# Attention and two expert layers on one core: the ordering pass books "engine free" and "result visible" apart

## The chip, the cores and the metric

The kernel runs on one core of a Trainium2 chip. The metric is the device time of one execution in microseconds; of several runs the median is given. The engines are PE (matrix multiply, with its weight loads PEld), DVE (vector), ACT (scalar), POOL and SP (which issues all DMAs here).

## What is computed

```python
def reference(**kwargs):
    # attention: q, k, v of (4, 8, 576, 64), a memory M_prev (4, 8, 64, 64), z_prev, a gate beta per head
    scores = scale * q @ k^T;  scores = where(causal, -1e9, scores);  a = softmax(scores)
    local = a @ v
    q_p = phi(q)                       # phi(x) = where(x > 0, x, exp(x) - 1) + 1
    mem_out = (q_p @ M_prev) / (q_p . z_prev + 1e-6)
    attn = g * mem_out + (1 - g) * local          # g = sigmoid(beta)
    x = attn.transpose(0, 2, 1, 3).reshape(2304, 512)
    h = x @ moe_w_in;  x = (h * tanh(softplus(h))) @ moe_w_out        # 512 -> 2048 -> 512
    h = x @ moe2_w_in; return (h * cos(h)) @ moe2_w_out               # 512 -> 2048 -> 512
```

## The kernel before

Nothing in the kernel is issued in the order in which the text stands. Each piece of work is a task (`add`, line 163): the engine or engines that may run it, a cost in microseconds, a function that issues its instructions, the tasks it depends on, a rank, the buffers it takes and uses. `arrange` (line 176) then plays a clock forward over all tasks. Whenever an engine is free at the moment `now`, it gets the task of lowest rank that is ready by then; ACT is asked before DVE, so a task that may run on either ("act/dve", mostly copies out of PSUM) goes to whichever is free first in this plan. The list that comes out is issued task by task, and each engine runs its own instructions in exactly that order; semaphores make a task wait for what it needs. So the planner's costs never make an instruction faster; they decide order and engine.

In the plan before, a task that starts at `now` occupies its engine until `now + cost`, and whoever depends on it may start 0.1 us (`SEM`) later, whichever engine it ran on. Costs are written beside each task, as formulas in the number of columns n for copies: `c_act(n) = 0.19 + 0.00082 n` and `c_dve(n) = 0.11 + 0.00106 n`. Changing ACT's table costs `TABLE`, changing PE's kind of matmul costs `SWITCH`.

The work has these stages:

- Attention in 16 pairs of heads (`pair`, rank 100 m). For each pair PE transposes q and k through PSUM (L400, tiles ptq and ptk), ACT or DVE copies them (L315 for ACT; L317, L319 for DVE), PE makes scores (L491, L495), DVE takes row maxima (L520), ACT exponentials with their sums (L536), DVE sums and scales (L563, L564, L572), PE transposes the probabilities (L587, tile t), ACT or DVE copies them (tile PT), PE multiplies with v (L654), ACT or DVE copies the result (tile xs), and SP stores it.
- Each f32 weight is split into two parts in 64 decodes (`decode_w`, L125 to L142): four DVE instructions and one of ACT each.
- The first half of the first layer's hidden units runs in nine blocks of 256 tokens (`block0`, L759 and L802), which start as soon as their tokens' attention is stored. One PSUM tile (tag h) holds the hidden values.
- The second half of them, and then the second layer, run in blocks of 384 tokens (`late`, L887, L967, L969), six blocks each. They have three hidden PSUM tiles, and the second matmul of a unit is ranked two or five units behind the first (`LAG`).

Until the first block takes its hidden tile, the planner fills PE with dummy matmuls (L303) where PE would be idle and was idle too often in the time before. Every buffer class has a number of slots (`slots_of`); a task that takes a slot waits until the users of the slot's last holder have ended.

Of the kernel before, what the change touches and what calls it, by code (L numbers as in the profile page):

```python
# [29 lines left out]
def tile_kernel(ctx: ExitStack, tc: tile.TileContext, q, k, v, M_prev, z_prev, beta,  # L30
# [13 lines left out]
    LAG = (2, 5)  # L44
# [110 lines left out]
            made[cls] = self.n + 1  # L155

    class Task:
        __slots__ = ("eng", "cost", "fn", "deps", "rank", "takes", "func", "mode", "lag", "end", "n", "size", "on")

    tasks = []  # L160
    slots_of = {}

    def add(eng, cost, fn, deps=(), rank=0.0, takes=(), uses=(), func=None, mode=0, lag=0.0, size=0):
        t = Task()
        t.eng, t.cost, t.fn, t.rank, t.takes = eng.split("/"), cost, fn, rank, list(takes)
        t.func, t.mode, t.lag, t.end, t.on, t.size = func, mode, lag, None, None, size
        t.deps = [d for d in deps if d is not None]
        for b in (*takes, *uses):
            b.users.append(t)
        tasks.append(t)  # L170
        return t

    SEM, SWITCH, TABLE, WAIT = 0.1, 0.12, 1.3, 2.5
    RATE, LAND = 160.0, 2.0

    def arrange():
        outs = {}
        for t in tasks:
            t.n = len(t.deps)
            for d in t.deps:  # L180
                outs.setdefault(id(d), []).append(t)
        ready = {e: [] for e in ("pe", "act", "dve", "pool", "sp", "host")}
        seen = 0

        def put(t):
            nonlocal seen
            at = max((d.end + (d.lag if t.eng[0] != "host" else 0.0) + SEM for d in t.deps), default=0.0)
            for e in t.eng:
                ready[e].append((t.rank, seen, at, t))
            seen += 1  # L190

        for t in tasks:
            if not t.n:
                put(t)
        held = {c: [None] * n for c, n in slots_of.items()}
        turn = {c: 0 for c in slots_of}
        free = {e: 0.0 for e in ready}
        func, mode, moved = "exp", 0, 0.0
        done = deque()
        now, order, left = 0.0, [], len(tasks)  # L200


        def at_free(b):
            if b.cls != "misc" and b.n != turn[b.cls]:
                return None
            o = held[b.cls][turn[b.cls] % len(held[b.cls])]
            if o is None:
                return 0.0
            at = 0.0
            for u in o.users:  # L210
                if u.end is None:
                    return None
                at = max(at, u.end + SEM)
            return at

        while left:
            nxt = None

            def later(x):
                nonlocal nxt  # L220
                if nxt is None or x < nxt:
                    nxt = x

            for e in ready:
                if free[e] > now:
                    later(free[e])
                    continue
                best = None
                for r in ready[e]:
                    rank, k, at, t = r  # L230
                    if t.on is not None:
                        continue
                    for b in t.takes:
                        f = at_free(b)
                        if f is None:
                            at = None
                            break
                        at = max(at, f)
                    if at is None:
                        continue  # L240
                    if t.func and t.func != func:
                        at += WAIT if t.func == "mish" else 0.0
                    if at > now:
                        later(at)
                        continue
                    key = (t.func == "mish" != func, rank, k) if func != "mish" else (t.func != "mish", rank, k)
                    if best is None or key < best[0]:
                        best = (key, r)
                if best is None:
                    if e == "pe" and t_warm.on and not turn["h"]:  # L250
                        while done and done[0][1] < now - 3.4:
                            done.popleft()
                        if sum(y - max(x, now - 3.4) for x, y in done) < 0.75 * 3.4:
                            t = Task()
                            t.eng, t.cost, t.fn, t.on, t.end = ["pe"], 0.12, f_dummy, "pe", now + 0.12
                            free[e] = t.end
                            done.append((now, t.end))
                            order.append(t)
                            later(t.end)
                    continue  # L260
                r = best[1]
                t = r[3]
                cost = t.cost[t.eng.index(e)] if isinstance(t.cost, tuple) else t.cost
                if e == "act" and t.func and t.func != func:
                    cost, func = cost + TABLE, t.func
                if e == "pe":
                    cost, mode = cost + (SWITCH if t.mode != mode else 0.0), t.mode
                t.on, t.end = e, now + cost
                free[e] = t.end
                if e == "pe":  # L270
                    done.append((now, t.end))
                if t.size:
                    moved = max(moved, t.end) + t.size / RATE
                    t.lag = moved - t.end + LAND
                for b in t.takes:
                    held[b.cls][turn[b.cls] % len(held[b.cls])] = b
                    turn[b.cls] += 1
                for x in t.eng:
                    ready[x] = [q_ for q_ in ready[x] if q_[3] is not t]
                order.append(t)  # L280
                left -= 1
                for d in outs.get(id(t), ()):
                    d.n -= 1
                    if not d.n:
                        put(d)
                later(t.end)
                if e == "host":
                    later(now)
            if left:
                assert nxt is not None, [(e, r[0], r[3].fn.__name__, [(b.cls, b.n, turn[b.cls]) for b in r[3].takes]) for e in ready for r in ready[e]][:40]  # L290
                now = max(now, nxt)
        return order
# [53 lines left out]
    def pair(m):  # L346
# [4 lines left out]
        R = 100.0 * m  # L351
        B_ = {n: Buf(n) for n in ("q", "k", "v", "z", "mv", "mn", "ph", "qT", "kT", "kd", "PT", "xs")}
# [98 lines left out]
        RP = R + 12  # L451
# [2 lines left out]
        p2 = add("dve", 0.82, f_p2, [p1], RP, [B_["ph"]], [B_["mn"], B_["q"]])  # L454
        p3 = add("dve", 0.82, f_p3, [p2, dz], RP, [], [B_["mn"], B_["ph"], B_["z"]])
        bden = Buf("den")
        p4 = add("dve", 1.2, f_p4, [p3, t_ginv], RP, [bden], [B_["mn"]])

        def slot(x):
# [41 lines left out]
            for c, i in enumerate(SLOTS[x]):  # L503
# [35 lines left out]
                for part in range(2 if nk > 512 else 1):  # L539
                    for j in range(2):  # L540
                        w = (main, nk - main)[part]
                        takes = [] if fst or bx else [bp]
                        t_e = add("act", 0.48 + 0.00083 * w, lambda e, j=j, part=part, f=f_ex: f(e, j, part), [t_m, fst], S_ + 2,
                                  takes, [bn] + ([] if takes else [bp]) + [bs if part == 0 else bx], func="exp")
                        exps[i, j, part] = t_e
                        fst = fst or t_e

# [19 lines left out]
            for c, i in enumerate(SLOTS[x]):  # L567
                n_ = START[i] + ROWS[i]
                for j in range(2):
                    def f_sl(e, c=c, i=i, j=j):  # L570
                        p_ = d["p", i][:, j, D:]
                        nc.vector.tensor_scalar(out=p_, in0=p_, scalar1=s["sm"][:, c, j:j + 1], scalar2=None, op0=ALU.mult)  # L572

                    scaled[i, j] = add("dve", 0.1 + n_ / 1920, f_sl, [t_sm], S_ + 3, [], [bp])
                colsof[i] = cols[i]
                ptof[i] = bp

# [258 lines left out]
    def late(bi, s0):  # L836
        p, j = blocks[bi]
        m = p - 1
# [34 lines left out]
        for k_, f in enumerate(fs):  # L873
# [6 lines left out]
            for half in range(2):  # L880
                def f_1(e, half=half, f=f, q_=q_, s=s):
# [3 lines left out]
                    for c in (2 * half, 2 * half + 1):  # L885
                        for pi, (a, e_) in enumerate(PASSES):
                            nc.tensor.matmul(q_["h"], w[:, a, 0, c * P:(c + 1) * P], x[:, e_, c, :],  # L887
                                             start=c == 0 and pi == 0, stop=c == NKC - 1 and pi == 2)

                pe_.append(add("pe", 1.05, f_1, [sp[half], *w_ready[m, f, 0], t_host, *pe_[-1:]], R, [bh] if half == 0 else [],  # L890
                               [bx, bw] + ([bh] if half else [])))

            def Gt(q_=q_, s=s):
# [64 lines left out]
            for c in range(na):  # L958
                def f_2(e, c=c, k_=k_, f=f, q_=q_):
# [4 lines left out]
                    for pi, (a, e_) in enumerate(PASSES):  # L964
# [3 lines left out]
                        else:  # L968
                            nc.tensor.matmul(o, G[:, a, c * P:(c + 1) * P], w[:, e_, 1, :], start=st, stop=sp_)  # L969

                prev[c] = add("pe", 0.53 if m == 0 else 0.7, f_2, [t, prev[c], *w_ready[m, f, 1]], R + 10 * LAG[m] - 5,
                              [ba[c]] if k_ == 0 else [], [bG, bw] + ([ba[c]] if k_ else []))
        RF = R0 + 10.0 * len(fs) + 10 * LAG[m]
        outs = []
# [155 lines left out]
```

## Time and profile before

| | before |
|---|---|
| median of 3 runs | 1081.99 us (1081.27 to 1083.91) |
| span of the profiled execution | 1080.1 us |
| PE busy | 1053.2 us (98%) |
| PEld busy | 938.7 us (87%) |
| DVE busy | 761.6 us (71%) |
| ACT busy | 570.1 us (53%) |

The span runs from the first to the last instruction of the one profiled execution; the profile gives no other time for that execution. Busy shares are averages over stages with different limits, and matmuls are pipelined, with modelled ends, so a busy PE isn't at its peak.

### The profile page before, as it was taken

Reading aid. Unit: us, or ns where it says so; the run is one execution under the profiler, and the core shown is the slowest. Engines: PE = TensorE matmul, PEld = TensorE weight load, DVE = VectorE, ACT = ScalarE, POOL = GpSimd, SP = SyncE. Lnnn points to the kernel's source line nnn. Section 1 sums busy time; section 2 is a strip of 40 time slices with the busy share of each in tenths; the row PEclk is TensorE's granted clock in tenths of the full one; section 3 lists DMA queues with packets and bytes.
Section 4 is the critical chain, followed back from the end, with each engine's and each line's share of the span. In section 5 each row is a group of like instructions: output and inputs, shape, how many; then the busy total and the mean of one; then the engine's idle time right before and its main releaser. Section 6 shows DMA issues by size and latency. Waiting matters only on the chain.

```text
span 1080.1 us, 17930 instructions
## 1 busy us (share of the span) xinstructions
PE 1053.2 (98%) x6938; PEld 938.7 (87%) x6938; DVE 761.6 (71%) x1694; ACT 570.1 (53%) x1279; POOL 3.8 (0%) x19
## 2 busy tenths in 40 slices
PE   8898999999999999999999999999999999999998
PEld 5666778788877899989999999998999999999997
DVE  6999997886787568757552228887666676766664
ACT  4676675676676443433323234766555555555544
POOL 1000000000000000000000000000000000000000
PEclk9999999999999999999999999999999999999999
DMA  6455423222322165446352216211000010000000
GB/s 165 114 132 161 113 55 103 69 70 67 100 69 59 44 204 156 137 135 205 102 183 88 89 59 187 79 38 59 1 30 30 1 59 2 30 30 1 30 1 30
DMA packets 112853, 88.73 MB, mean 82 GB/s; under 512 B 65792, under 2 KB 103680, under 8 KB 112768
## 3 DMA queue, kind: packets, MB, share of 16 engines
q1 hardware_dynamic: 112768, 87.58, 27.1%
q8 instruction: 55, 0.90, 0.3%
q14 instruction: 30, 0.25, 0.1%
HBM read 68.69 MB, written 18.87 MB: 81 GB/s over the span
## 4 chain that ended last, share of the span: by engine, by line
PE 88%; DVE 7%; ACT 3%; issue 1%; POOL 0%; ACTq 0%; POOLq 0%; DVEq 0%
PE h L887 28%; PE acc L969 18%; PE acc L967 9%; PE h L759 9%; PE acc L802 9%; PE pv L654 5%; PE t L587 4%; PE s L491 3%; DVE nm L520 2%; DVE p L572 1%; PE warm L303 1%; ACT p L536 1%; PE ptq L400 1%; ACT PT L315 1%; PE ptk L400 1%
## 5 line engine op out<-in xcount | busy, mean ns | idle before, releaser
L887 PE MATMUL h<-x,w 128*128 128x384 f32 x1728 | 345.0, 337 | 1.6 <-ACT g L903 1.6
L887 PEld LDWEIGHTS h<-x,w 128*128 128x128 f32 x1728 | 307.4, 188 | 17.2 <-ACT g L903 1.8
L969 PE MATMUL acc<-w,G 128*128 128x512 f32 x864 | 228.4, 393 | 0.0
L969 PEld LDWEIGHTS acc<-w,G 128*128 128x128 f32 x864 | 160.0, 188 | 22.1
L954 DVE TENSOR_TENSOR G<-g,G 128x384 fp32r<-128x384 f32 x144 | 79.8, 555 | 100.2 <-ACT G L315 99.6
L759 PE MATMUL h<-x,w 128*128 128x256 f32 x864 | 127.7, 288 | 4.6 <-DVE g L317 4.2
L802 PE MATMUL acc<-G,w 128*128 128x256 f32 x864 | 129.7, 289 | 1.1 <-ACT o L315 0.7
L759 PEld LDWEIGHTS h<-x,w 128*128 128x128 f32 x864 | 111.4, 191 | 9.0 <-DVE g L317 5.2
L315 ACT ACTIVATE G<-g 128x384 fp32r<-128x384 f32 (+1 forms) x152 | 81.2, 535 | 66.6 <-DVE g L938 35.8
L802 PEld LDWEIGHTS acc<-G,w 128*128 128x128 f32 x864 | 111.9, 191 | 4.0 <-ACT o L315 1.4
L967 PE MATMUL acc<-G,w 128*128 128x384 f32 x576 | 112.6, 336 | 0.0
L536 ACT ACTIVATE p<-s,nm 128x64 f32<-128x64 f32 (+4 forms) x160 | 81.3, 515 | 40.0 <-DVE nm L520 26.2
L967 PEld LDWEIGHTS acc<-G,w 128*128 128x128 f32 x576 | 100.9, 188 | 0.0
L931 ACT ACTIVATE n<-n 128x384 f32<-128x384 f32 x96 | 49.9, 521 | 63.5 <-DVE n L927 63.5
L903 ACT ACTIVATE g<-h 128x384 f32<-128x384 f32 x48 | 23.4, 491 | 113.1 <-PE h L887 112.2
L587 PE MATMUL t<-ident,p 128*128 128x128 f32 (+1 forms) x480 | 73.7, 277 | 7.8 <-ACT PT L315 3.7
L520 DVE TENSOR_REDUCE nm<-s 128x2 f32<-128x1024 f32 (+4 forms) x80 | 62.2, 790 | 23.5 <-PE s L495 16.4
L915 DVE TENSOR_SCALAR u<-hs 128x384 f32<-128x384 f32 x96 | 34.5, 359 | 54.6 <-ACT hs L315 51.9
L938 DVE TENSOR_TENSOR g<-n,hs 128x384 f32<-128x384 f32 x96 | 53.2, 555 | 26.3 <-ACT n L934 26.2
L587 PEld LDWEIGHTS t<-ident,p 128*128 128x128 f32 (+1 forms) x480 | 52.3, 140 | 18.5 <-ACT PT L315 7.8
L315 ACT ACTIVATE hs<-h 128x384 f32<-128x384 f32 x96 | 47.0, 490 | 39.3 <-PE h L887 36.6
L315 ACT ACTIVATE PT<-t 128x256 f32<-128x256 f32 (+3 forms) x97 | 43.4, 466 | 42.0 <-PE t L587 41.5
(91 smaller groups left out, 1243.6 us busy)
## 6 DMA issues: line engine op xcount, KB each, us to landing
raw<-in_moe_w_in_dram SPq DMA_DIRECT2D x32, 512.0 KB, 4.3
raw<-in_moe_w_out_dram SPq DMA_DIRECT2D x32, 512.0 KB, 3.8
k<-in_k_dram SPq DMA_DIRECT2D x32, 144.0 KB, 2.8
x1d<-xs SPq DMA_DIRECT2D x32, 144.0 KB, 2.1
xad<-o SPq DMA_DIRECT2D x9, 512.0 KB, 3.7
x2d<-o SPq DMA_DIRECT2D x6, 768.0 KB, 3.6
x<-x2d SPq DMA_DIRECT2D x6, 768.0 KB, 4.2
out_dram<-o SPq DMA_DIRECT2D x18, 256.0 KB, 2.0
```

Source lines behind the costliest of these rows:

```text
L315: nc.scalar.activation(dst, src, AF.Copy, scale=1.0 if scale is None else scale)
L520: nc.vector.tensor_reduce(out=s["nm"][:, c], in_=s["sp"][i], axis=AX.X, op=ALU.max, negate=True)
L536: nc.scalar.activation(d["p", i][:, j, D + lo:D + hi], src, AF.Exp, bias=s["nm"][:, c, j:j + 1], scale=1.0, accum_out=s["sm"][:, 1 if part ...
L587: nc.tensor.transpose(ps[:, at:at + r], d["p", i][0:r, h, j * P:(j + 1) * P], ident[0:r, 0:r])
L654: nc.tensor.matmul(o[h * D:(h + 1) * D, z_ - lo:w], vt[:, h, j - 1, :] if j else d["mv"][:, h, :], PT[:, c + z_:c + hi], start=j == 0, sto ...
L759: nc.tensor.matmul(h[:, half // 2], w[:, a, 0, c * P:(c + 1) * P], x[:, e_, c, :], start=c == 0 and pi == 0, stop=c == NKC - 1 and pi == 2)
L802: nc.tensor.matmul(t[:, c], w[:, a, 1, n * P:(n + 1) * P], G[:, e_, half], start=f == 0 and pi == 0 and c == 0, stop=f == NFH - 1 and pi == 2,
L887: nc.tensor.matmul(q_["h"], w[:, a, 0, c * P:(c + 1) * P], x[:, e_, c, :], start=c == 0 and pi == 0, stop=c == NKC - 1 and pi == 2)
L938: nc.vector.tensor_tensor(out=q_["g"], in0=q_["n"], in1=q_["hs"], op=ALU.mult)
L954: ENG[e].tensor_tensor(out=q_["G"][:, 1], in0=q_["g"], in1=q_["G"][:, 0].bitcast(F32), op=ALU.subtract)
L967: nc.tensor.matmul(o, w[:, a, 1, c * P:(c + 1) * P], G[:, e_, :], start=st, stop=sp_)
L969: nc.tensor.matmul(o, G[:, a, c * P:(c + 1) * P], w[:, e_, 1, :], start=st, stop=sp_)
```

## The change

The planner's clock books two moments for each task instead of one: when its engine is free for the next task (`NEXT`, `over`) and when others see the result (`TAIL`, `SEM`). On ACT and DVE the engine is free 0.10 and 0.09 us before the task's end, and others see the end 0.035 us later. On PE the engine is free at the task's end, and others see it 0.16 + 0.035 us later. A buffer read by a DMA counts as free only when the DMA has landed (`u.lag`). Some costs change: exponentials, scalings, the denominator, dummies and the late matmuls. No instruction is edited.

```diff
-    def add(eng, cost, fn, deps=(), rank=0.0, takes=(), uses=(), func=None, mode=0, lag=0.0, size=0):
+    def add(eng, cost, fn, deps=(), rank=0.0, takes=(), uses=(), func=None, mode=0, lag=0.0, size=0, over=0.0):
...
-    SEM, SWITCH, TABLE, WAIT = 0.1, 0.12, 1.3, 2.5
+    SEM, SWITCH, TABLE, WAIT = 0.035, 0.12, 1.28, 2.5
     RATE, LAND = 160.0, 2.0
+    TAIL = {"pe": 0.16, "act": 0.0, "dve": 0.0, "sp": 0.0, "host": -SEM}
+    NEXT = {"pe": 0.0, "act": -0.1, "dve": -0.09, "sp": 0.0, "host": 0.0}
...
-                at = max(at, u.end + SEM)
+                at = max(at, u.end + u.lag + SEM)
...
-                            t.eng, t.cost, t.fn, t.on, t.end = ["pe"], 0.12, f_dummy, "pe", now + 0.12
+                            t.eng, t.cost, t.fn, t.on, t.end = ["pe"], 0.112, f_dummy, "pe", now + 0.112
...
-                t.on, t.end = e, now + cost
-                free[e] = t.end
+                t.on, t.end = e, now + cost + TAIL[e]
+                free[e] = now + cost + NEXT[e] + (t.over if e != "pe" else 0.0)
                 if e == "pe":
-                    done.append((now, t.end))
+                    done.append((now, free[e]))
...
-                later(t.end)
+                later(free[e])
...
-        p4 = add("dve", 1.2, f_p4, [p3, t_ginv], RP, [bden], [B_["mn"]])
+        p4 = add("dve", 1.27, f_p4, [p3, t_ginv], RP, [bden], [B_["mn"]])
...
-                        t_e = add("act", 0.48 + 0.00083 * w, lambda e, j=j, part=part, f=f_ex: f(e, j, part), [t_m, fst], S_ + 2,
-                                  takes, [bn] + ([] if takes else [bp]) + [bs if part == 0 else bx], func="exp")
+                        t_e = add("act", 0.35 + 0.00083 * w, lambda e, j=j, part=part, f=f_ex: f(e, j, part), [t_m, fst], S_ + 2,
+                                  takes, [bn] + ([] if takes else [bp]) + [bs if part == 0 else bx], func="exp", over=-0.01)
...
-                    scaled[i, j] = add("dve", 0.1 + n_ / 1920, f_sl, [t_sm], S_ + 3, [], [bp])
+                    scaled[i, j] = add("dve", 0.215 + n_ / 1920, f_sl, [t_sm], S_ + 3, [], [bp], over=0.005)
...
-                pe_.append(add("pe", 1.05, f_1, [sp[half], *w_ready[m, f, 0], t_host, *pe_[-1:]], R, [bh] if half == 0 else [],
+                pe_.append(add("pe", 1.042, f_1, [sp[half], *w_ready[m, f, 0], t_host, *pe_[-1:]], R, [bh] if half == 0 else [],
...
-                prev[c] = add("pe", 0.53 if m == 0 else 0.7, f_2, [t, prev[c], *w_ready[m, f, 1]], R + 10 * LAG[m] - 5,
+                prev[c] = add("pe", 0.52 if m == 0 else 0.692, f_2, [t, prev[c], *w_ready[m, f, 1]], R + 10 * LAG[m] - 5,
```

## Rows read from the trace of the kernel before

**Rows 1.** The page: span, and busy time of each engine.

```profile
span 1080.1 us, 17930 instructions
...
PE 1053.2 (98%) x6938; PEld 938.7 (87%) x6938; DVE 761.6 (71%) x1694; ACT 570.1 (53%) x1279; POOL 3.8 (0%) x19
```

**Rows 2.** Stretches: length, busy (instructions) of PE, PEld, DVE, ACT, POOL, clock, DMA.

```profile
20.00:105.80 85.80, 76.27 (x633) 52.48 (x633) 81.30 (x217) 57.55 (x179) 0.00 (x0) 1.00 0.51 133
105.80:160.00 54.20, 50.46 (x429) 40.32 (x430) 52.03 (x122) 37.05 (x98) 0.00 (x0) 1.00 0.33 88
160.00:480.00 320.00, 314.50 (x2615) 275.89 (x2614) 231.55 (x543) 175.77 (x427) 0.00 (x0) 1.00 0.34 97
480.00:1066.00 586.00, 585.19 (x3087) 549.55 (x3088) 381.23 (x774) 286.27 (x544) 0.00 (x0) 1.00 0.19 63
```

**Rows 3.** The same for 20 to 160 us, line L303 alone: PE, PEld.

```profile
20.00:160.00 140.00, 20.55 (x149) 14.31 (x149) 1.00 0.44 116
```

**Rows 4.** PE in order of time, 96 to 107 us: start, duration, instruction.

```profile
104.55 1.15 PE L303 MATMUL warm<-zeros,ident_b 128*128 128x256 bf16 x9
105.84 0.99 PE L759 MATMUL h<-x,w 128*128 128x256 f32 x6 [0.15 <-PE warm L303]
```

**Rows 5.** DVE in order of time, 60 to 75 us.

```profile
64.06 0.69 DVE L317 COPY PT<-t 128x512 f32<-128x512 f32 x1
64.67 0.42 DVE L125 TENSOR_SCALAR dec<-raw 128x512 int32<-128x512 int32 x1
65.00 0.82 DVE L435 SCALAR_TENSOR_TENSOR ph<-q,mn 128x640 f32<-128x640 f32 x1
...
68.52 0.17 DVE L445 SCALAR_TENSOR_TENSOR den<-den,ginv 128x10 f32<-128x10 f32 x1
68.72 0.22 DVE L449 RECIPROCAL den<-den 128x10 f32<-128x10 f32 x1
```

**Rows 6.** ACT in order of time, 60 to 75 us.

```profile
60.19 0.60 ACT L315 ACTIVATE PT<-t 128x512 f32<-128x512 f32 x1 [0.41 <-PE t L587]
60.69 0.38 ACT L315 ACTIVATE qT<-ptq 128x256 f32<-128x256 f32 x1
...
70.63 0.63 ACT L536 ACTIVATE p<-s,nm 128x448 f32<-128x448 f32 x1 [0.24 <-DVE nm L520]
71.16 0.19 ACT L536 ACTIVATION_READ_ACCUMULATOR p<-s,nm 128x1 f32 x1
71.26 0.63 ACT L536 ACTIVATE p<-s,nm 128x448 f32<-128x448 f32 x1
```

**Rows 7.** 20 to 160 us, line L536 alone (exponentials on ACT).

```profile
20.00:160.00 140.00, 38.57 (x150) 1.00 0.44 116
```

**Rows 8.** 20 to 160 us, line L572 alone (scalings on DVE).

```profile
20.00:160.00 140.00, 21.64 (x66) 1.00 0.44 116
```

**Rows 9.** 20 to 160 us, line L317 alone (copies on DVE).

```profile
20.00:160.00 140.00, 19.36 (x38) 1.00 0.44 116
```

**Rows 10.** 20 to 160 us, line L315 alone (copies on ACT).

```profile
20.00:160.00 140.00, 38.66 (x96) 1.00 0.44 116
```

**Rows 11.** Who PE waited for, 20 to 160 us: us, times, longest.

```profile
PE t L587 <- ACT PT L315: 3.7, 7, 1.4
PE h L759 <- DVE g L317: 2.4, 3, 1.0
```

**Rows 12.** The page's DMA issues: KB each, us from issue to landing.

```profile
xad<-o SPq DMA_DIRECT2D x9, 512.0 KB, 3.7
```

**Rows 13.** The chain that ended last, in order of time.

```profile
853.27 1.40 PE acc L969 x6
857.49 1.40 PE acc L969 x6
```

**Rows 14.** Groups of DVE instructions, 20 to 105.8 us: busy, mean ns.

```profile
L125 DVE TENSOR_SCALAR dec<-raw 128x512 int32<-128x512 int32 x10 | 4.2, 418 | 0.0
L128 DVE SCALAR_TENSOR_TENSOR dec<-raw,dec 128x512 int32<-128x512 int32 x10 | 6.8, 683 | 0.0
```

More of the change, by code (lines that the diff above doesn't have):

```diff
@@ L157, in tile_kernel @@
     class Task:
-        __slots__ = ("eng", "cost", "fn", "deps", "rank", "takes", "func", "mode", "lag", "end", "n", "size", "on")
+        __slots__ = ("eng", "cost", "fn", "deps", "rank", "takes", "func", "mode", "lag", "end", "n", "size", "on", "over")
     tasks = []
     slots_of = {}
-    def add(eng, cost, fn, deps=(), rank=0.0, takes=(), uses=(), func=None, mode=0, lag=0.0, size=0):
+    def add(eng, cost, fn, deps=(), rank=0.0, takes=(), uses=(), func=None, mode=0, lag=0.0, size=0, over=0.0):
         t = Task()
         t.eng, t.cost, t.fn, t.rank, t.takes = eng.split("/"), cost, fn, rank, list(takes)
-        t.func, t.mode, t.lag, t.end, t.on, t.size = func, mode, lag, None, None, size
+        t.func, t.mode, t.lag, t.end, t.on, t.size, t.over = func, mode, lag, None, None, size, over
         t.deps = [d for d in deps if d is not None]
```

## The prediction

> **What bounds the kernel now.** I read the page first. PE is busy for 1053.2 of the span's 1080.1 us [rows 1], so at first sight 27 us are left to win. Then the stretches [rows 2], because the kernel has stages with different limits. From 480 to 1066 us (both expert layers in blocks of 384 tokens) PE is busy for 585.19 of 586 us: there an order of instructions can win 0.8 us at most. From 160 to 480 us, where attention and the 256-token blocks run together, PE is busy for 314.5 of 320 us. The room lies ahead of 160 us. From 20 to 160 us DVE is busy for 81.30 + 52.03 = 133.3 of 140 us, 95%, while ACT is busy for 57.55 + 37.05 = 94.6 us, so ACT has 45 us to spare. PE shows 126.7 us there, but 149 of its instructions are the dummy matmuls of L303 [rows 3], issued only because the planner had nothing else for it; the first real matmul of a token block comes at 105.84 us, right behind such dummies [rows 4]. So the length of the first 160 us is set by DVE, and PE takes over as the limit behind it. What shortens DVE's list there by one microsecond brings PE's full stage forward by up to one microsecond.
>
> **The change part by part.** No instruction of the computation is added or removed, and no DMA either. The planner's figures change, so the order on every queue can change, as can the engine of each task that may run on ACT or DVE (a PSUM copy), and the number of dummies. The cost is therefore that of another order, and the first question is which bookings were wrong.
>
> *Until the engine is free.* The figure now booked is 0.10 us (ACT) and 0.09 us (DVE) before the task's end. The trace shows these overlaps. A DVE copy of 512 starts at 64.06, lasts 0.69, and its successor starts at 64.67, so 0.08 before its end; the one behind that starts 0.09 before the end of its forerunner [rows 5]. On ACT a copy that starts at 60.19 and lasts 0.60 is followed at 60.69, 0.10 early [rows 6]. The Trainium skill (VectorE: DVE Perf Modes, The DRAIN you can't avoid) says that the next DVE operation doesn't start until the pipe has emptied, though it adds that one which isn't held starts earlier. By the first half of that rule the new DVE figure would be too short in every task and the plan would overload DVE, an outcome that stands below as the slower rival; the rows show the overlap, so I don't take it into the sum.
>
> *Exponentials.* An exponential of width w was booked at 0.48 + 0.00083 w until ACT is free, and is now booked at 0.35 - 0.10 - 0.01 + 0.00083 w, 0.24 less. For 448 columns that is 0.85 us before and 0.61 us after; the trace has 71.26 - 70.63 = 0.63 us, accumulator read included [rows 6]. The old figure was badly long, the new one is right. From 20 to 160 us there are 150 instructions on that line, two for each exponential, so 75 exponentials and 75 x 0.24 = 18.0 us [rows 7]. The other instructions of ACT in these stretches, 179 + 98 = 277 less the 150 [rows 2], are 127, and 127 x 0.10 = 12.7 us. So ACT is booked 30.7 us shorter than before, on a stretch of 140 us.
>
> *DVE's bookings.* 217 + 122 = 339 instructions [rows 2] by 0.09 us would be 30.5 us, but the scaling of the probabilities is booked 0.115 + 0.005 = 0.12 us longer, and there are 66 of these [rows 8]: 7.9 us back. That leaves 22.6 us at most. A task that holds two or three instructions (a slot's sums, the denominator) takes the 0.09 only once; were a hundred of the 339 such seconds and thirds, 9 us more would drop out and 13.6 us be left.
>
> *What moves.* A copy that may run on either goes to the engine that the plan finds free, ACT being asked first. ACT's list shrinks by 30.7, DVE's by 22.6, a difference of 8.1 us. A copy moved from DVE to ACT closes that difference by its time on both. On DVE a 512-copy holds the engine for 64.67 - 64.06 = 0.61 us, and over the 38 copies of the line in this stretch the mean duration is 19.36 / 38 = 0.51 us [rows 9], less 0.08 for the overlap 0.43 us; on ACT the 96 of its line take 38.66 / 96 = 0.40 us [rows 10]. So 8.1 / (0.43 + 0.40) = some 10 of the 38 copies move, and DVE, the limit, is relieved of 10 x 0.43 = 4.3 us. ACT takes on 10 x 0.40 = 4 us, which hide in its 45 us of idle time; were that gone, they would come back as waits of the copies' readers on PE. The bounds of this unknown are no copy moved (0 us) and, with a fall of 13.6 us for DVE, (30.7 - 13.6) / 0.83 = 21 copies (9 us). I take 4.3 us, since 22.6 us is counted from rows and the hundred is an estimate. A move in the other direction isn't excluded (below).
>
> *Until others see the result.* From ACT and DVE it falls from 0.10 to 0.035 us. A DVE operation on its own forerunner's result ends at 68.52 + 0.17 = 68.69 and the next starts at 68.72, 0.03 us later [rows 5], so the new figure fits. From PE the lag grows from 0.10 to 0.195 us, for PE's own next task too. The chip doesn't wait there, as PE takes its matmuls one behind the other; in the plan, another chain's task slides into that gap, which it did at 0.10 us as well, because 0.73 us of work doesn't fit into either gap. Cost 0, covered by the second chain; without that cover the plan alone has a hole. PE's waits on copies, which a better lag could shorten, are 3.7 + 2.4 us in the two largest rows from 20 to 160 us [rows 11]; PE isn't the limit there, so they count nothing.
>
> *Stores.* A buffer that a store reads is now free only when the store has landed. The largest is 3.7 us for xad [rows 12] on a tile reused one block later; the 320 us from 160 to 480 hold about nine blocks, some 35 us each. Cost 0; if a next block were at its copy at once, up to 3.7 us for a block.
>
> *Late units.* The bookings fall by 1 to 2%. A unit of the last layer takes 857.49 - 853.27 = 4.22 us [rows 13], booked 4.20 before (2 x 1.05 + 3 x 0.70) and 4.16 now. PE is full there, so the order has nothing to win; three tiles for the hidden layer and a lag of two or five units cover the chains behind it. Cost 0, and at most the 0.8 us of idle time to win. The end of the kernel (1066 to 1080.1) is a row of matmuls, then copies and stores that are fixed: 0.
>
> **Sum.** From the profiled span: 1080.1 - 4.3 = 1075.8 us. The median of the runs is 1081.99, 1.9 us above the span, which I add: 1077.7 us.
>
> **The Trainium skill** (Perfetto Trace Analysis, Identifying the Most-Contended Engine) holds matmul busy time to be a poor measure and weight-load busy time a better one. From 20 to 160 us the trace has 52.48 + 40.32 = 92.8 us of weight loads [rows 2], so by that rule PE's room there is 47 us where matmul time leaves 13 us. The sum would be the same by either, since DVE sets the pace; the rule only makes a larger gain possible, which is the third rival.
>
> **The rivals.** *No measurable difference*: DVE's bookings fall nearly as much as ACT's, so the split of the copies stays and only their order changes. For it speaks that the plan is greedy and the ranks are the same; against it, that the exponentials alone give ACT 18 us. Time 1082.0, within 2.5 us.
>
> *Slower*: the copies go the other way. The formula for a DVE copy isn't changed: 0.11 + 0.00106 n, so 0.65 for 512, and with the new 0.09 off 0.56, while the trace has 0.61. ACT's is 0.61 - 0.10 = 0.51, and the trace has 0.50. So the plan now believes DVE free 0.05 us too soon behind each of its copies, and DVE is asked whenever ACT is inside an exponential. If 10 more copies land on DVE before 160 us, DVE's list grows by 4.3 us: 1086.3 us. It decides from 3.25 / 0.43 = 8 copies on. Against it: DVE is behind its list anyway, so its being free is the rarer case.
>
> *Larger gain*: the order on DVE changes and not its load. From 20 to 105.8 us about ten weight decodes lie in its list [rows 14], each 0.42 + 3 x 0.69 less four overlaps of 0.08, 2.2 us. If four of them slip behind the work of the first pairs, the first block can start 4 x 2.2 = 8.8 us sooner, and DVE has 88 us of room from 160 to 480 us for them: 1073.2 us, and 1069 with the copies on top. Against it: the blocks need these weights soon after.
>
> **How the numbers follow.** About 0.3% (3.2 us) is what a measurement of this kernel can tell from no change, so faster is below 1078.7 and slower above 1085.2. Chances: forecast 0.42 (own range 1075.0 to 1080.0), larger gain 0.12, no difference 0.27, slower 0.19. Some 0.06 of the forecast lies within 0.3%, so faster is 0.48, same 0.33, slower 0.19. The range reaches from the larger gain with most of the copies on top, 1070.0, to the slower rival, 1086.3.
>
> **What would show it.** Right: fewer than 38 copies on DVE's line between 20 and 160 us (28 or so), ACT busier there by 4 us, DVE still above 90%, the first matmul of L759 some 3 to 5 us before 105.84, fewer dummies than 149 behind 20 us, and the stretch of full PE time from then to the end as long as now. Wrong: as many or more copies on DVE; a first block that starts earlier and then waits for weights or for its one hidden tile; PE idle time above 5.5 us in the stage that ends near 480 us; or new idle time in the late units.

## The result and the profile after

The change made the kernel slower by 0.9%: 1091.37 us median (1090.39 to 1093.06, 4 runs) against 1082.33 for the kernel before (4 runs); ratio 1.0088, 95% interval 1.0073 to 1.0102. The forecast was 1077.7, and the range ended at 1086.3. The profiled execution took 1093.06 us at a mean granted clock of 0.995, its span is 1091.3 us.

The page of the changed kernel, beside [rows 1]:

```profile
span 1091.3 us, 17849 instructions
...
PE 1058.0 (97%) x6892; PEld 937.1 (86%) x6892; DVE 718.3 (66%) x1608; ACT 607.6 (56%) x1363; POOL 3.9 (0%) x19
```

Its stretches, columns as in [rows 2]:

```profile
20.00:105.80 85.80, 72.45 (x570) 49.17 (x567) 79.37 (x207) 54.87 (x174) 0.00 (x0) 0.94 0.51 133
105.80:160.00 54.20, 51.87 (x437) 40.36 (x438) 53.01 (x133) 39.24 (x102) 0.00 (x0) 1.00 0.36 95
160.00:480.00 320.00, 314.12 (x2590) 272.38 (x2587) 218.20 (x523) 176.14 (x430) 0.00 (x0) 1.00 0.32 95
480.00:1066.00 586.00, 582.57 (x3088) 546.08 (x3087) 346.61 (x693) 315.68 (x608) 0.00 (x0) 1.00 0.19 64
```

DVE is as full as before from 20 to 160 us (79.37 + 53.01 = 132.4 us, before 133.3). New is the clock, 0.94 in the first of these stretches. The copies (lines L319 on DVE and L317 on ACT, 20 to 160 us), beside [rows 9, 10]:

```profile
20.00:160.00 140.00, 17.72 (x36) 0.96 0.45 118
```

```profile
20.00:160.00 140.00, 39.83 (x96) 0.96 0.45 118
```

Two of 38 copies left DVE, where ten were forecast, and ACT has the same 96. The two are copies of the token blocks (g<-h: five on DVE before; three there and two on ACT now). Then the marks of the stages, from the lines of the dummies and of the token blocks' two matmuls (count; shortest, median and longest ns; first and last start; forms):

```profile
L305 PE MATMUL warm<-zeros,ident_b x172: 270/273/421, 2.0 to 110.5; 128*128 128x256 bf16 x172
```

```profile
L761 PE MATMUL h<-x,w x864: 277/283/388, 116.8 to 473.5; 128*128 128x256 f32 x173
```

```profile
L804 PE MATMUL acc<-G,w x864: 277/283/387, 140.9 to 486.8; 128*128 128x256 f32 x173
```

The last of these in the kernel before:

```profile
L802 PE MATMUL acc<-G,w x864: 277/283/387, 131.6 to 478.9; 128*128 128x256 f32 x173
```

In the kernel before the first block started at 105.8, and the last matmul of the blocks at 478.9. So the first block is 11.0 us late and the blocks' end 7.9 us. From there to the end it took 1080.1 - 478.9 = 601.2 us before and 1091.3 - 486.8 = 604.5 us now, 3.3 us more. 7.9 + 3.3 = 11.2 us is the difference of the two spans.

The clock, in steps of 4 us (columns as above):

```profile
24.00:28.00 4.00, 4.00 (x21) 3.17 (x19) 3.17 (x8) 1.71 (x4) 0.00 (x0) 0.57 0.00 0
...
80.00:84.00 4.00, 2.63 (x14) 1.71 (x14) 3.16 (x9) 2.72 (x13) 0.00 (x0) 0.78 0.33 74
84.00:88.00 4.00, 3.95 (x19) 3.45 (x19) 2.71 (x11) 1.89 (x4) 0.00 (x0) 0.50 0.33 98
88.00:92.00 4.00, 3.80 (x29) 2.51 (x29) 3.60 (x9) 2.19 (x6) 0.00 (x0) 0.87 0.11 38
```

So there are two dips in this execution, one at 24 and one that begins within 80 to 84 us, where PE is thinly used (14 matmuls, busy for 2.63 of 4 us). Behind that PE is granted 0.50 of its clock, 1.2 instead of 2.4 GHz. In the profile before, every step up to 124 us shows 1.00.

The rounding task of the last layer (`f_k`), in the page's groups of the changed kernel:

```profile
L922 ACT ACTIVATE u<-u,magic 128x384 f32<-128x384 f32 x86 | 52.9, 615 | 35.5 <-DVE u L917 35.4
```

86 of 96 run on ACT, where they take 0.615 us; before, 17 did, and 79 ran on DVE at 0.361 us:

```profile
L922 DVE TENSOR_SCALAR u<-u x79: 352/361/364, 681.9 to 1067.8; 128x384 f32<-128x384 f32 x79
```

### The profile page after: what moved, and what is told of

It reads as the page before. It is cut to its first block, busy times and chain, and to the rows that moved or that the text cites. A ratio compares the mean times of both kernels' runs of the same rounds, so it can differ in the third digit from the quotient of the medians.

```text
span 1091.3 us, 17849 instructions
## 1 busy us (share of the span) xinstructions
PE 1058.0 (97%) x6892; PEld 937.1 (86%) x6892; DVE 718.3 (66%) x1608; ACT 607.6 (56%) x1363; POOL 3.9 (0%) x19
## 4 chain that ended last, share of the span: by engine, by line
PE 61%; DVE 22%; ACT 12%; issue 3%; DMA 0%; POOL 0%; SPq 0%; ACTq 0%; DVEq 0%; POOLq 0%
PE h L889 18%; PE acc L971 9%; PE acc L969 9%; PE acc L804 8%; PE h L761 7%; DVE nm L522 4%; PE t L589 3%; ACT p L538 3%; ACT n L936 3%; PE pv L656 3%; DVE n L929 2%; ACT u L922 2%; DVE g L940 2%; ACT n L933 2%; DVE G L956 2%
## 5 line engine op out<-in xcount | busy, mean ns | idle before, releaser
L761 PE MATMUL h<-x,w 128*128 128x256 f32 x864 | 130.8, 289 | 2.4 <-ACT g L317 1.1
L538 ACT ACTIVATE p<-s,nm 128x320 f32<-128x320 f32 (+4 forms) x160 | 81.6, 518 | 38.0 <-DVE nm L522 24.7
L589 PE MATMUL t<-ident,p 128*128 128x128 f32 (+1 forms) x480 | 76.8, 287 | 10.0 <-DVE PT L319 5.1
L317 ACT ACTIVATE G<-g 128x384 fp32r<-128x384 f32 (+1 forms) x154 | 81.2, 527 | 9.1 <-DVE g L940 7.1
L929 DVE SCALAR_TENSOR_TENSOR n<-u,hs 128x384 f32<-128x384 f32 x96 | 53.5, 557 | 48.4 <-ACT u L922 47.8
L589 PEld LDWEIGHTS t<-ident,p 128*128 128x128 f32 (+1 forms) x480 | 55.2, 146 | 23.0 <-DVE PT L319 8.1
L922 ACT ACTIVATE u<-u,magic 128x384 f32<-128x384 f32 x86 | 52.9, 615 | 35.5 <-DVE u L917 35.4
L140 ACT ACTIVATE w<-dec 128x512 fp32r<-128x512 f32 x64 | 39.9, 628 | 55.6 <-DVE dec L131 53.9
```

The costliest lines, as they stand in the source:

```text
L317: nc.scalar.activation(dst, src, AF.Copy, scale=1.0 if scale is None else scale)
L538: nc.scalar.activation(d["p", i][:, j, D + lo:D + hi], src, AF.Exp, bias=s["nm"][:, c, j:j + 1], scale=1.0, accum_out=s["sm"][:, 1 if part ...
L589: nc.tensor.transpose(ps[:, at:at + r], d["p", i][0:r, h, j * P:(j + 1) * P], ident[0:r, 0:r])
L761: nc.tensor.matmul(h[:, half // 2], w[:, a, 0, c * P:(c + 1) * P], x[:, e_, c, :], start=c == 0 and pi == 0, stop=c == NKC - 1 and pi == 2)
L929: nc.vector.scalar_tensor_tensor(out=q_["n"], in0=q_["u"], scalar=(-TWO_PI_HI, -TWO_PI_LO)[z_], in1=(q_["n"] if z_ else q_["hs"]), op0=ALU ...
```

## Experiments

Each kernel was timed beside the kernel before on the same chip; the brackets give the ratio to it and its 95% interval. The theories: **1** the release half (engine free early, exponentials, scalings and denominator) sets off the loss; **2** the result lags, PE's above all (2a the tail, 2b the short lag of ACT and DVE, 2c the hole that the plan books between two dependent PE tasks); **3** fewer dummies let the clock fall; **4** luck, any other order costs as much; **5** a plan booked to the edge; **6** the rounding on ACT.

**First: one part taken out at a time.**

```diff
no_release:   -NEXT = {... "act": -0.1, "dve": -0.09 ...}   +0.0, 0.0; old costs of exp, scaling, p4; over 0
no_lags:      -SEM 0.035, TAIL pe 0.16                      +SEM 0.1, TAIL pe 0.0
no_landing:   -at = max(at, u.end + u.lag + SEM)            +at = max(at, u.end + SEM)
more_dummies: -... < 0.75 * 3.4                             +... < 0.9 * 3.4
```

> The change without its engine-release half: engines count as busy until the task's end, with the old costs of exponentials, scalings and denominator; the result lags, the store landing and the PE constants stay changed. Theory 1 (the shorter ACT and DVE bookings let attention run ahead of the blocks and leave less useful PE work from 160 to 380 us): back to 1081 to 1085 us. Theory 2 (the PE lag of 0.195 us in the plan does it): stays at 1089 to 1093. Theory 3 (fewer dummies, so a lower granted clock and a late pair 3): as many dummies as before and full clock would give some 1087, fewer would stay at 1091.

> The change without its result-lag half: 0.1 us for every result and no tail for PE; the engine-release half stays. Theory 1: stays at 1089 to 1093 us. Theory 2: back to 1081 to 1085. Theory 3: goes with the dummies and the granted clock of the first 120 us.

> The change without the landing of stores in a buffer's release. All three theories: no more than 3 us from 1091.4, as the order changes only where a buffer is read by a store; a larger change would say that the order alone, whatever its reason, is worth that much.

> The change, with the dummies' threshold raised from 0.75 to 0.9 of the time before, so that more of them are issued. Theory 3: the granted clock stays at 1.00 ahead of 120 us and the time falls to 1086 to 1088. Theories 1 and 2: within 2 us of 1091.4.

Measured: without the release half 1080.54 us (0.9981 of the kernel before, 0.9972 to 0.9991), without the lags 1083.91 (1.0013, 1.0001 to 1.0025), without the landing 1090.56 (1.0077, 1.0062 to 1.0092), with more dummies 1098.17 (1.0141, 1.0122 to 1.0159). Neither half is bad alone: taking out either returns 7 to 11 us, so theories 1 and 2 both got what they had asked for, and neither alone explains it. The landing is harmless. Theory 3 as the whole cause falls: with 266 dummies the profiled execution has a clock of 1.000 and still takes 1095.48 us, and the median is the highest of all kernels here. No theory had expected it above 1093.4.

**Second: smaller parts.**

```diff
no_tail:  -TAIL = {"pe": 0.16, ...                      +TAIL = {"pe": 0.0, ...
pe_to_pe: in put(): SEM                                 +(-TAIL["pe"] if d.on == "pe" and t.eng[0] == "pe" else SEM)
no_next:  -NEXT act -0.1, dve -0.09; over -0.01, 0.005  +0.0 each; the new costs stay
old_exp:  -add("act", 0.35 + 0.00083 * w, ... over=-0.01  +add("act", 0.48 + 0.00083 * w, ... over=0.0
```

> The change with PE's tail of 0.16 us left out, everything else kept: PE's results are booked visible 0.035 us after the task. Theory 2a (the long PE lag, on top of the release half, is the harmful piece): 1081 to 1085 us, near the 1083.9 of the run without both lags. Theory 2b (the shorter lag of ACT and DVE is): stays at 1089 to 1093.

> The change, but a PE task that depends on a PE task may start at once in the plan; the tail of 0.16 us and 0.035 us hold for the other engines alone. Theory 2c (the harm is the hole of 0.195 us that the plan books between dependent PE tasks, which the chip doesn't have): 1080 to 1084 us, as without a tail or better. Theory 2a in its other form (the harm lies in the later copies of ACT and DVE): stays at 1089 to 1093.

> The change with ACT and DVE booked busy until their task's end (no 0.10 and 0.09 us back), the new exponential, scaling and denominator costs kept. Theory 1a (the release figures set off the middle loss of some 3.5 us): 1081 to 1085 us. Theory 1b (the cheaper exponential does): stays at 1088 or above, since exponentials stay 0.13 us cheaper than before the change.

> The change with the old exponential cost (0.48 + 0.00083 w, no 0.01 back), the rest kept, so that ACT is booked some 0.14 us longer in each exponential. Theory 1b: attention no longer runs 13 us of PE work ahead by 320 us, and the time falls to 1083 to 1087. Theory 1a: within 3 us of 1091.4.

Measured: 1089.64 (1.0067, 1.0050 to 1.0084), 1085.15 (1.0029, 1.0018 to 1.0041), 1086.79 (1.0046, 1.0031 to 1.0061) and 1095.52 (1.0125, 1.0110 to 1.0140). PE's tail is not the harmful piece by itself (2a falls, and the time is what 2b expected), and the old exponential doesn't bring the time down (1b falls). Without the release figures the time falls by 4.6 us, which is short of what 1a expected. Closing the hole returns 6 us, to just above 2c's range. Yet that kernel loses time elsewhere. Its PE at the end of the token blocks, in order of time, and then by steps:

```profile
466.26 3.04 PE L761 MATMUL h<-x,w 128*128 128x256 f32 x24
471.73 0.40 PE L804 MATMUL acc<-G,w 128*128 128x256 f32 x1 [2.44 <-ACT G L317]
472.86 5.28 PE L804 MATMUL acc<-G,w 128*128 128x256 f32 x23 [0.73 <-DVE G L781]
```

```profile
472.00:476.00 4.00, 3.27 (x15) 3.14 (x15) 0.80 (x2) 0.00 (x0) 0.00 (x0) 0.50 0.02 4
476.00:480.00 4.00, 3.31 (x20) 3.02 (x20) 0.00 (x0) 0.76 (x2) 0.00 (x0) 0.65 0.00 0
```

PE waits 2.44 us for a copy on ACT, and then 23 matmuls take 5.28 us where 24 took 3.04 just before: the wait is paid a second time, in clock.

**Third: changes without a meaning.** The result lag 0.09 and 0.11 us in the kernel before, 0.03 and 0.04 us in the changed one.

> The kernel before with the result lag booked at 0.09 instead of 0.10 us, a difference with no meaning of its own that still gives another order on every engine. Theory 4 (any other order costs as much as the change, as the old one was picked by luck): slower by 5 to 12 us. Theories 1 and 2 (the release half and the PE lag have effects of their own): within 3 us of 1082.

> The same with 0.11 us. Theory 4: slower by 5 to 12 us. Theories 1 and 2: within 3 us of 1082.

> The changed kernel with the result lag booked at 0.03 instead of 0.035 us. Theory 4: somewhere between 1081 and 1095, as far off the changed kernel as the orders of the kernel before are off theirs. Theories 1 and 2: within 3 us of 1091.4.

> The same with 0.04 us. Theory 4: somewhere between 1081 and 1095. Theories 1 and 2: within 3 us of 1091.4.

Measured: 1079.80 (0.9986, 0.9976 to 0.9996) and 1093.41 (1.0108, 1.0093 to 1.0123); 1093.28 (1.0101, 1.0085 to 1.0118) and 1090.62 (1.0085, 1.0070 to 1.0100). Theory 4 was right for one step of the kernel before and wrong for the other: a hundredth of a microsecond in a booking is worth between -2 and +12 us. The changed kernel stays at 1090 to 1094 through steps of half that size. In the slow one of the kernel before, PE's useful work is 6.3 us behind at 140 us, most of it lost since 120 us (how this is counted stands below), and its clock reads

```profile
132.00:136.00 4.00, 3.52 (x16) 2.56 (x16) 3.93 (x10) 1.57 (x5) 0.00 (x0) 0.50 0.33 127
```

**Fourth: margin, rounding, remaining costs.**

```diff
after_margin:   in put(): SEM  +SEM + (0.3 if t.eng[0] == "pe" and d.on in ("act", "dve") else 0.0)
margin_no_hole: the same, and the edit of pe_to_pe
round_on_dve:   -add("act/dve", (0.49, 0.36), f_k   +add("act/dve", (0.62, 0.36), f_k
true_costs:     the same, and c_dve 0.11 -> 0.15, f_kd on dve 0.40 -> 0.46
```

> The change, with 0.3 us more booked between the end of an ACT or DVE task and a PE task that needs it. Theory 5 (with exact figures the plan puts PE's tasks at the earliest moment, so each small delay on the chip makes PE, which keeps its order, wait; the old longer figures were a margin): 1082 to 1086 us, with the 3 to 5 us of useful PE work lost between 160 and 380 us back. Theory 4 (luck): anywhere from 1080 to 1095.

> The same margin, and PE tasks on PE results may start at once in the plan. Theories 2c and 5 together: 1079 to 1083 us. If the loss of 5 us at the step to the late blocks, seen without the hole, stays: 1084 to 1087. Theory 4: anywhere from 1080 to 1095.

> The change, with the rounding task of the last layer booked at its traced 0.62 us on ACT instead of 0.49, so that it goes back to DVE; nothing ahead of the last layer changes. Theory 6 (the rounding on ACT lengthens the chain of a late unit and costs the 1 to 2 us lost behind 500 us): 1089.5 to 1090.5. Otherwise 1091.4 as before.

> The change with the copies on DVE booked 0.04 us longer, as the trace has them, the rounding at 0.62 us on ACT and the small key copies at 0.46 on DVE. If the remaining wrong bookings were the cause of the 9 us: 1080 to 1084. Theory 5 (exactness itself is the trouble): 1088 to 1093. Theory 4: anywhere from 1080 to 1095.

Measured: 1093.06 (1.0088, 1.0068 to 1.0107), 1088.88 (1.0056, 1.0041 to 1.0071), 1089.16 (1.0058, 1.0039 to 1.0077), 1089.52 (1.0057, 1.0039 to 1.0075). Theory 5 falls: margin alone returns nothing. Margin and no hole together miss both ranges that were named for them (1079 to 1083 and 1084 to 1087). The remaining wrong costs aren't the cause of the bulk. The booking of the rounding returns somewhat more than theory 6 expected; whether by theory 6's reason is looked at below.

**Last: the hole by size, and in the kernel before.** The hole set to 0.10 us in the change, and to 0 in the kernel before.

> The kernel before, but a PE task that depends on a PE task may start at once in the plan; all other bookings are the old ones. Theory 2c (the hole harms wherever it stands): 1077 to 1081 us, which would beat both kernels. Theory 4 (luck of an order and of the clock): 1080 to 1094.

> The change, but between dependent PE tasks 0.10 us as before it, 0.195 us for the other engines alone. Theory 2c by size: useful PE work at 470 us between that of the change (6 us behind the kernel before) and that without the hole (1 us behind), time 1085 to 1089. If only the exact zero helps: 1089 to 1093, as with the change. Theory 4: anywhere from 1080 to 1095.

Measured: 1093.34 (1.0087, 1.0058 to 1.0116; 1088.5 to 1096.4) and 1090.77 (1.0074, 1.0058 to 1.0091). The hole of 0.10 us gives the useful work that 2c expected, but not the time. In the kernel before, closing the hole did harm, so it isn't harmful wherever it stands: 2c falls as a general rule. The trace shows where this kernel loses most of it. At 470 us its useful work is some 2 us behind; then PE waits as it did above,

```profile
474.11 0.38 PE L802 MATMUL acc<-G,w 128*128 128x256 f32 x1 [2.44 <-ACT G L315]
```

its clock reads 0.57 from 476 to 480 us, and the last matmul of its blocks starts at 485.9 us instead of 478.9.

## Why the prediction was wrong

**The clock has a price of its own, and the sum had no term for it.** Executions of one and the same program show it. Of the kernel before, 35 with a mean granted clock of 1.000 took 1081.2 to 1082.1 us, and 17 with 0.998 took 1083.7 to 1084.2: 2.4 us for 0.002 of the clock, about the PE time that is lost (0.002 x 1082 = 2.2 us). The four executions of the changed kernel had 0.995 to 0.998. The one with 0.998 took 1090.39 us, 6 to 7 more than the kernel before at 0.998; so 2 to 3 of the 9 us are clock, and the rest is order. The kernel with the rounding booked at 0.62 us has the same order on PE as the changed one throughout, and on DVE and ACT up to 712 us; in its profiled execution the clock fell in the first dip too, but not in the second:

```profile
80.00:84.00 4.00, 2.39 (x20) 1.72 (x18) 3.90 (x13) 2.57 (x11) 0.00 (x0) 1.00 0.32 74
84.00:88.00 4.00, 3.80 (x28) 2.32 (x27) 4.00 (x12) 3.56 (x8) 0.00 (x0) 1.00 0.44 131
```

```profile
L804 PE MATMUL acc<-G,w x864: 277/283/388, 137.9 to 483.9; 128*128 128x256 f32 x173
```

Its last matmul of a token block starts at 483.9 instead of 486.8 us: this one dip costs 2.9 us. The order doesn't decide alone whether a dip comes: PE is as thinly used here (2.39 of 4 us) and keeps its clock. The prediction named fewer dummies than 149 behind 20 us as a sign of success. They came (112), and the dips with them. Of the twelve kernels here with 159 to 194 dummies in all, every profiled execution has a dip ahead of 90 us; of the eight with 218 to 266, one has. That goes together; that one brings the other is likely but not shown, and more dummies made this kernel slower.

**"What moves" failed, and so did the step from DVE's list to PE.** Ten copies were to leave DVE ahead of 160 us and two did; DVE's time in the stage fell by 0.9 us and not by 4.3. The difference of 8.1 us between the two engines' bookings was read as copies that change engine. But in the plan a copy goes to the engine that is free when it comes ready, and both engines became free earlier. (The sum took the overlap off DVE's 0.51 us and not off ACT's 0.40; with 0.30 it gives 11 copies and 4.8 us, no other forecast.) Where the copies did leave, the second step failed as well: that each microsecond off DVE's list brings PE's full stage forward by up to one. With the release figures alone taken out (`no_next`), nine copies fewer ran on DVE from 20 to 160 us,

```profile
20.00:160.00 140.00, 15.09 (x29) 0.98 0.45 116
```

and DVE was busy there for 127.3 us instead of 133.3. But the first block started at 109.4 us, 3.6 us later than in the kernel before, at a clock of 1.00 up to then, and the last matmul of the blocks at 485.2. Nor does the first block's start set the blocks' end: with the lag at 0.03 us the first block starts at 107.1, 9.7 us ahead of the changed kernel, and the last matmul of the blocks at 486.5. The slower rival had the sign right by luck and the mechanism wrong: on balance no copy went to DVE.

**"Late units: cost 0, the order has nothing to win" failed.** It had something to lose: behind the blocks' end the changed kernel takes 3.3 us longer. `f_k` was booked at 0.49 us on ACT and takes 0.615. In the kernel before ACT takes 17 of the 96, and 24 in the two changed kernels that book ACT busy until the task's end; with ACT free 0.10 us sooner in the plan it takes 86, as ACT is asked first. With the booking at 0.62, 65 of the 92 behind 680 us stay on ACT and 27 go to DVE, and at an equal clock the time falls from 1093.06 to 1090.5 (0.995) and from 1090.39 to 1087.8 (0.998): 2.5 us. The late part then takes 1086.0 - 483.9 = 602.1 us, against 604.5 for the changed kernel. But the rounding on ACT isn't what costs this by itself, so theory 6's reason fails. Without the hole, 89 roundings run on ACT,

```profile
L922 ACT ACTIVATE u<-u,magic x89: 600/617/620, 682.0 to 1072.0; 128x384 f32<-128x384 f32 x89
L804 PE MATMUL acc<-G,w x864: 275/283/581, 129.3 to 484.6; 128*128 128x256 f32 x173
```

and the late part takes 1085.1 - 484.6 = 600.5 us, less than in the kernel before; without both lags it is 84 roundings and 601.3 us. With the lag at 0.04 us, where the hole stands, it is 85 and 602.1 us. So neither the rounding on ACT nor the hole is enough, and what makes the rest of the 3.3 us isn't settled.

**"Until others see the result: cost 0" can't stand either.** I counted PE's useful work: each matmul done by a moment, at one fixed price for its line (about the planner's cost of its task by the number of its matmuls, 0.122 us for a block's), less the same sum of the kernel before. At 470 us the changed kernel is 6.2 us behind, with a hole of 0.10 us 3.8, without a hole 0.6, with margin and no hole 1.8, without both lags 1.0; without the release half it is 1.2 ahead. These figures are good to about half a microsecond. At an equal clock of 0.995 the three sizes of the hole, 0.195, 0.10 and 0, give 1093.1, 1090.0 to 1091.0 and 1087.1 us. So in this plan the hole carries 6 us at equal clock. They aren't all where the count at 470 us puts them: by the marks 486.8 - 484.6 = 2.2 us lie ahead of the blocks' end and 604.5 - 600.5 = 4.0 us behind it, since between 470 us and the blocks' end the kernel without the hole loses 5 us again. A loss of 4 to 6 us there stands in all four kernels whose hole was made smaller: PE's last matmuls of the blocks wait for ACT's copy (2.44 us without the hole in the change, with margin, and in the kernel before; 1.00 us with 0.10), and behind the wait the clock reads 0.50 to 0.65 from 476 to 480 us; in no other kernel does it fall there. Without the hole the plan puts 24 matmuls of one kind behind one another, as the rows above show, and nothing is left to cover the last copy. So closing the hole has a price at this one step in the kernel before too, where it made the kernel slower by 4.6 us at an equal clock (1088.5 against 1083.9, both at 0.998). What the hole costs ahead of 470 us, beside the release figures and not in the kernel before, isn't settled: every edit reorders thousands of instructions.

**The account of the 11.2 us between the two profiled executions.** The dip at 84 us 2.9 (a pair of executions of one order); the dip at 24 us about 1.7 (0.43 x 4 us of clock, an estimate); order ahead of the blocks' end the rest of 7.9, that is 3.3; behind it 3.3, of which the booking of the rounding returns 2.4. The 3.3 us ahead of the blocks' end are what the clock leaves over, so order. At 470 us they are gone without the hole and without either half. That they are more than luck is likely, as six close relatives of the changed kernel (both lag steps, the margin, the true costs, no tail, no landing) all lie between 1089.5 and 1093.3 us, but not shown: one meaningless step moved the kernel before by more than the whole change did.

**What was right.** PE is full behind 160 us, DVE is busy for 95% ahead of it in both kernels, though that alone doesn't set the stage's length; the landing costs nothing that these runs can tell; the overlap of 0.08 to 0.10 us is real. Of the signs of being wrong two came: from 160 to 480 us PE is idle for 5.9 us (5.5 before), and from 480 to 1066 us for 3.4 (0.8 before), though 2.3 of this is the step behind the blocks, which has moved into that stretch. That figures nearer to the trace make a better plan was the unspoken step, and the runs contradict it.

## What to carry to other kernels

A greedy planner's costs are not a measure that improves with accuracy: before one version is called better, step a booking by a meaningless 0.01 us and see how far the time moves, which here was up to 12 us. When some figures of an engine are corrected, look at what the others now attract: the one left wrong (the rounding) moved from DVE to ACT. A count at one moment can mislead: what an order wins by then, it can lose again at the next change of stage. Where PE is nearly full, look at the granted clock in steps of some microseconds and compare executions of equal clock, or a reordering is charged with what the clock did. Two kernels here are slightly faster than the one before, by 0.14% (the lag at 0.09 us) and 0.19% (the change without its release half), neither beyond what such a step gives by luck.

## What was not expected of the hardware

The clock isn't the same from one execution of a program to the next: the kernel before has 1.000, 0.999 and 0.998 in turn, and its time follows in steps, 1081.2 to 1082.1, 1082.5 to 1082.8 and 1083.7 to 1084.2 us. From kernel to kernel the mean clock alone doesn't give the time so closely: with the lag at 0.03 us, 0.997 took 1093.5 to 1093.6 us and 0.995 took 1093.0. Two kernels with one order on every engine up to 712 us differed at 84 us: one kept its clock, the other fell to 0.50. A wait of 2.44 us on PE was followed by two steps of 4 us at 0.50 and 0.65 of the clock, in which 23 matmuls took 5.28 us instead of about 3.
